# Forward 47-point stage on the quarters of the matrix array: groups of four points, plain float32

## The chip, the cores and the metric

The kernel runs on one core of one Trainium2 chip. A core has five engines with an instruction queue each: TensorE (PE in the profile, with its weight loads as PEld), VectorE (DVE), ScalarE (ACT), GpSimd (POOL) and SyncE (SP, which here only issues transfers). The metric is the device time of one execution in microseconds. The kernel before takes 2449.47 us (median of 3 runs, 2446.99 to 2450.57).

## The reference

Eight sequences `x[b]` of 3008 tokens by 256 channels are Fourier transformed along the tokens, mixed with a complex 256x256 matrix, shrunk towards zero, and transformed back. What comes out passes a token-mixing and a channel-mixing layer.

```python
X = np.fft.rfft(x, axis=1)
Yr = Xr @ w_r - Xi @ w_i + b_r
Yi = Xr @ w_i + Xi @ w_r + b_i
Yr = np.sign(Yr) * np.maximum(np.abs(Yr) - lam, 0.0)   # Yi alike
y = np.fft.irfft(Y, n=x.shape[1], axis=1)
...
h = np.maximum(xt @ w_tok1, 0.0) @ w_tok2
u = x + h.transpose(0, 2, 1)
h2 = np.maximum(u @ w_ch1, 0.0) @ w_ch2
return (u + h2).astype(np.float32)
```

## The kernel before

**Units.** 3008 is 47 times 64, so the transform is done as 47-point transforms at each of 64 residues n2 (stage one), and then 64-point transforms. The batches are worked in five units: batch 0 alone, batch 1 alone, and then three pairs (`UNITS`). A unit's work on the spectrum, `spectral(u)`, runs while the channel layer of the unit before it, `channel(n)`, keeps TensorE busy. Unit 0 has its own beginning, `begin`, in which stage one is done another way (`stage1_turned`).

**Stage one** (`dft47`, `stage1`). Since the input is real, each residue needs only sums and differences of rows j and 47-j: 24 cosine terms from the sums and 24 sine terms from the differences. Five residues ("points") make a group of 5 times 24 = 120 partitions, and one 120x120 block-diagonal constant `f1` does all five, once with cosines (i = 0) and once with sines (i = 1). 64 points need 13 groups. A group is 512 columns wide in a unit of two batches, 256 in unit 1. For each group: SP loads `x` (three buffers, loaded three groups ahead); POOL (DVE in unit 1) makes the sums and DVE the differences, `sd`; ACT copies `sd` into a rounded float32 `xh` (type float32r, which the matrix unit takes in one pass) and DVE makes the rest `xl = sd - xh`; then `mm3` (L185 to L188) does three float32r products each for cosines and sines, six in all, into two PSUM banks (one bank in unit 1); ACT copies the banks to `a` (L257) and issues its store to `a_d` in DRAM (L259). All matrix products whose lines are L186, L187 and L188 are such triples; plain float32 products stand at other lines, such as L337, L451, L475, L517 and L751.

**What sets the order.** The code records instructions through generators. `channel(n)` yields after each of its 14 slices, and the loop at the end then takes as many steps of `spectral(u + 1)` as a pace asks for: every step yields its cost (0.7 us per batch of a stage-one group), the pace is work left in `spectral` over work left in `channel`. A scheduling layer then sets the final place of each instruction in its engine's queue from operands and buffers; it may move products of one group apart. PSUM has four banks in rotation (`bank`) which stage one shares with the first product of the channel layer (`ph`), the mixing products and others. `make_w` (L337), which only the beginning uses, is the one place before the change where products use a part of the array: its constant has 64 columns, so its four float32 products of a step write the upper or the lower half of a bank, two and two.

## Time and profile before

| | before |
|---|---|
| median of 3 runs | 2449.47 us (2446.99 to 2450.57) |
| span of the profiled execution, first to last instruction | 2442.4 us |
| median less span, what lies around the span | 7.1 us |
| instructions | 31613 |
| PE busy | 2420.4 us, 99% |
| DVE, ACT, POOL busy | 1103.6, 875.3, 305.2 us |
| granted TensorE clock | 1.000 |
| stage-one rows on TensorE outside unit 0 and the weights | 234 with 512 columns, 78 with 256 |

The page gives the profiled execution's span and no other time of that execution, so 7.1 us is taken for what lies around the span in every run. A row of the profile has the line in the kernel, the engine, the operation and "out<-in" by the program's names with buffer numbers left out (a PSUM bank `p1` shows as `p`). One float32r product is one MATMUL row; one plain float32 product is two MATMUL rows, with a weight load each. A matmul's shown duration goes on after the next has begun, so what a product costs is read from the distance between starts, not from its duration.

### The profile page before, as it was taken

The page shows a single profiled execution, that of the slowest core. Times are in us where ns is not written, and L with a number is a line of the kernel's source. Part 1 is how long each engine was busy: PE and PEld are TensorE (multiplying, and loading weights), DVE is VectorE, ACT ScalarE, POOL GpSimd, SP SyncE. Part 2 cuts the span into 40 slices and gives each one's busy share as a digit, 9 for nine tenths or more (in the row PEclk, how much of TensorE's full clock was granted, in tenths as well). Part 3 has the DMA queues.
Part 4 walks back from the last instruction along what each step waited for, and adds up shares of the span by engine and source line. Part 5 has one row for each costly group of instructions (what it writes and reads, how often), then busy time and mean ns, then how long its engine had stood idle before and what let it go on. Part 6 is the DMA issues. An engine that isn't in the chain of part 4 may idle for free.

```text
span 2442.4 us, 31613 instructions
## 1 busy us (share of the span) xinstructions
PE 2420.4 (99%) x12848; PEld 2114.3 (87%) x12848; DVE 1103.6 (45%) x1680; ACT 875.3 (36%) x1580; POOL 305.2 (12%) x259
## 2 busy tenths in 40 slices
PE   8999999999999999999999999999999999999999
PEld 7778999988888888888888898888888888888887
DVE  7986655454445444433344353444334333232332
ACT  6764444443333343333333253333333222222221
POOL 0000223122222011111111120111111000000000
PEclk9999999999999999999999999999999999999999
DMA  8864335542324352223322363232321212112110
GB/s 216 254 210 141 102 111 160 167 138 93 100 86 131 112 170 72 60 80 91 89 75 69 98 177 105 68 99 76 93 67 37 70 50 64 59 49 81 37 56 18
DMA packets 143998, 246.07 MB, mean 101 GB/s; under 512 B 10293, under 2 KB 97677, under 8 KB 143853
## 3 DMA queue, kind: packets, MB, share of 16 engines
q1 hardware_dynamic: 114073, 190.57, 26.4%
q10 hardware_dynamic: 29780, 53.49, 7.0%
q8 instruction: 101, 1.65, 0.3%
q14 instruction: 44, 0.36, 0.0%
HBM read 159.74 MB, written 84.28 MB: 100 GB/s over the span
## 4 chain that ended last, share of the span: by engine, by line
PE 93%; DMA 2%; DVE 2%; ACT 1%; SPq 1%; issue 0%; POOL 0%; ACTq 0%; DVEq 0%; POOLq 0%
PE ph L186 10%; PE ph L187 10%; PE ph L188 10%; PE po L188 10%; PE po L186 10%; PE po L187 10%; PE pu L751 5%; PE px L451 3%; PE pm L186 2%; PE pm L188 2%; PE pm L187 2%; PE pu L186 2%; PE pu L187 2%; PE pu L188 2%; PE gp L186 2%; PE gp L188 2%
## 5 line engine op out<-in xcount | busy, mean ns | idle before, releaser
L790 DVE SCALAR_TENSOR_TENSOR hlo<-ph,hh 128x512 fp32r<-128x512 f32 (+4 forms) x588 | 392.0, 667 | 640.0 <-ACT hh L789 635.8
L789 ACT ACTIVATE hh<-ph 128x512 fp32r<-128x512 f32 (+4 forms) x588 | 340.9, 581 | 822.3 <-PE ph L188 820.2
L186 PE MATMUL ph<-uh,w 128*128 128x512 f32 (+4 forms) x1176 | 455.7, 388 | 0.9 <-DVE hlo L790 0.9
L187 PE MATMUL ph<-ul,w 128*128 128x512 f32 (+4 forms) x1176 | 449.1, 382 | 0.0
L186 PE MATMUL po<-hh,w2h 128*128 128x512 f32 (+4 forms) x1176 | 448.5, 381 | 0.0
L188 PE MATMUL ph<-uh,w 128*128 128x512 f32 (+4 forms) x1176 | 448.5, 381 | 0.0
L187 PE MATMUL po<-hlo,w2h 128*128 128x512 f32 (+4 forms) x1176 | 447.9, 381 | 0.0
L188 PE MATMUL po<-hh,w2l 128*128 128x512 f32 (+4 forms) x1176 | 447.8, 381 | 0.0
L188 PEld LDWEIGHTS ph<-uh,w 128*128 128x128 f32 x1176 | 220.8, 188 | 39.5
L187 PEld LDWEIGHTS po<-hlo,w2h 128*128 128x128 f32 x1176 | 220.9, 188 | 38.6
L186 PEld LDWEIGHTS po<-hh,w2h 128*128 128x128 f32 x1176 | 220.8, 188 | 38.5
L188 PEld LDWEIGHTS po<-hh,w2l 128*128 128x128 f32 x1176 | 220.8, 188 | 38.4
L186 PEld LDWEIGHTS ph<-uh,w 128*128 128x128 f32 x1176 | 221.2, 188 | 35.5 <-DVE hlo L790 1.3
L187 PEld LDWEIGHTS ph<-ul,w 128*128 128x128 f32 x1176 | 221.3, 188 | 34.0 <-DVE ul L760 0.2
L140 DVE TENSOR_TENSOR xtl<-xf,xth 128x768 fp32r<-128x768 f32 x84 | 80.5, 958 | 208.7 <-ACT xth L137 208.7
L186 PE MATMUL pm<-wmh,xth 128*128 128x256 f32 x504 | 144.4, 287 | 1.1 <-ACT xth L137 1.1
L758 ACT COPY uf<-pu 128x470 f32<-128x470 f32 (+23 forms) x188 | 62.7, 376 | 228.1 <-PE pu L751 228.1
L140 POOL TENSOR_TENSOR yl<-z,yh 128x512 fp32r<-128x512 f32 x72 | 92.9, 1290 | 408.6 <-ACT yh L137 408.6
L188 PE MATMUL pm<-wmh,xtl 128*128 128x256 f32 x504 | 142.4, 283 | 0.0
L187 PE MATMUL pm<-wml,xth 128*128 128x256 f32 x504 | 142.3, 283 | 0.0
L751 PEld LDWEIGHTS pu<-g,b 96*128 96x128 f32 x1024 | 130.8, 191 | 3.4
L454 POOL TENSOR_TENSOR xf<-xf 128x256 f32<-128x256 f32 x84 | 69.0, 821 | 484.8 <-ACT xf L453 483.3
(130 smaller groups left out, 3216.3 us busy)
## 6 DMA issues: line engine op xcount, KB each, us to landing
wt<-wt_d SPq DMA_DIRECT2D x28, 940.0 KB, 5.6
x<-in_x SPq DMA_DIRECT2D x39, 480.0 KB, 4.4
a<-a_d SPq DMA_DIRECT2D x36, 512.0 KB, 3.8
b_d<-bt ACTq DMA_DIRECT2D x36, 512.0 KB, 3.3
out<-o SPq DMA_DIRECT2D x34, 512.0 KB, 2.8
a_d<-a ACTq DMA_DIRECT2D x36, 480.0 KB, 3.4
wt<-wt_d SPq DMA_DIRECT2D x21, 752.0 KB, 5.2
b<-b_d SPq DMA_DIRECT2D x32, 480.0 KB, 6.3
```

What stands on the lines that cost most here:

```text
L140: lo_eng.tensor_tensor(out=lo, in0=src, in1=hi.bitcast(F32), op=ALU.subtract)
L186: PE.matmul(out, lhsT=wh, rhs=xh, start=start, stop=False)
L187: PE.matmul(out, lhsT=wh, rhs=xl, start=False, stop=False)
L188: PE.matmul(out, lhsT=wl, rhs=xh, start=False, stop=stop)
L451: PE.matmul(pt[:, o:o + 128], lhsT=x, rhs=f2cols(2 * kp + ab), start=True, stop=True)
L454: (V if plain else G).tensor_tensor(out=xf[:, 0], in0=xf[:, 1], in1=xf[:, 2], op=ALU.add)
L751: PE.matmul(pt[:, s * TOKS:(s + 1) * TOKS], lhsT=b2[:, s, cs], rhs=g2[:, 0 if s0 + s == 0 else 1], start=False, stop=s == k - 1)
L758: S.copy(out=ufs[m][:, ct, lo - at:hi - at], in_=pt[:, lo - c0:hi - c0])
L789: S.activation(out=hh, in_=pt, func=AF.Relu)
L790: V.scalar_tensor_tensor(out=hlo, in0=pt, scalar=0.0, in1=hh.bitcast(F32), op0=ALU.max, op1=ALU.subtract)
```

## The change

Stage one of units 1 to 4 works in groups of four points: 16 groups in place of 13. The four points are two pairs r = 0, 1. A pair's 48 rows lie at partitions 0 to 47 and 64 to 111, and the constant `fq` has 48 rows and 64 columns, so that a product uses a quarter of the 128x128 array: r picks the upper or the lower half of the rows, i (cosines or sines) the left or right half of the columns. The two r write two banks, the two i the two halves of a bank. The four products of a group (a "quad" from here on) are plain float32 from `sd` as it is; the split into `xh` and `xl` goes, and with it the constants `f1r`. A group's load is two transfers, its store two. Sums and differences are made one group ahead of the products where it was two. The step's cost in the pacing is 0.47 per batch where it was 0.7, and `left_s` 68.7 where it was 70.3. Stage one of unit 0 and of the weights keeps groups of five; their last group now overlaps the one before it, since the host's array has no padding.

```diff
-NG = 13
-GS = 5
+NG, GS = 16, 4
+NG5, GS5 = 13, 5
...
+    fq = np.zeros((2, 2, KH, 2, 2, 32))
+    for n in range(2):
+        fq[:, n, :, 0, n, :KH] = f1[:KH, 0, :KH]
+        fq[:, n, :, 1, n, :KH] = f1[:KH, 1, :KH]
...
-    f1r = const.tile([120, 2, 2, 128], F32R, name="f1r")
+    fq = const.tile([128, 2, 64], F32, name="fq")
...
-    split(f1r[:, 0], f1r[:, 1], f1w[:, :2], S, V)
...
-    def split_x(sd, w):
-        xh, xl = hl([120, 2, w], "xh"), hl([120, 2, w], "xl")
-        split(xh, xl, sd, S, V)
-        return xh, xl
+    def load_q(src, nb):
+        x = ld([128, 2, nb, C], "x")
+        for r in range(2):
+            n = (64, 2 * KH)[r]
+            DMA.dma_start(out=x[r * 64:r * 64 + n], in_=src[r * 2 * KH:r * 2 * KH + n])
+        return x.rearrange("q i b c -> q i (b c)")[:112]
+
+    def stage1_quads(x, dst, g, w, eng):
+        sd = t4([112, 2, w], "sd")
+        eng.tensor_tensor(out=sd[:, 0], in0=x[:, 0], in1=x[:, 1], op=ALU.add)
+        V.tensor_tensor(out=sd[:, 1], in0=x[:, 0], in1=x[:, 1], op=ALU.subtract)
+        yield
+        a = ev([128, 2, w], "a")
+        pts = [bank("p1") for _ in range(2)]
+        for i in range(2):
+            for r in range(2):
+                ks = slice(r * 64, r * 64 + 2 * KH)
+                PE.matmul(pts[r][i * 64:(i + 1) * 64, :w], lhsT=fq[ks, i], rhs=sd[ks, i], start=True, stop=True)
+        for r in range(2):
+            S.copy(out=a[:, r], in_=pts[r][:, :w])
+        rows = dst.rearrange("(i g r n) k w -> i g (n k) r w", i=2, r=2, n=2)
+        for i in range(2):
+            PUT.dma_start(out=rows[i, g, :, :, :w], in_=a[i * 64:i * 64 + 2 * KH])
+
+    def dft_quads(load, dst, w, eng):
+        xs = [load(g) for g in range(3)]
+        yield 0.0
+        ahead = []
+        for g in range(NG + 1):
+            if g < NG:
+                if g + 3 < NG:
+                    xs.append(load(g + 3))
+                q = stage1_quads(xs[g], dst, g, w, eng)
+                xs[g] = None
+                next(q)
+                ahead.append(q)
+            if g >= 1:
+                for _ in ahead.pop(0):
+                    pass
+                yield 0.47 * w / C
...
-        yield from dft47(p.load_unit, p.a, p.w, 3, V if u == 1 else G)
+        yield from dft_quads(p.load_unit, p.a, p.w, V if u == 1 else G)
...
+            DMA.dma_start(out=fq, in_=io["fq"])
...
-            left_s = len(UNITS[u + 1]) * 70.3 - done
+            left_s = len(UNITS[u + 1]) * 68.7 - done
```

**TensorE, unit 3, between the second half of one channel chunk's products.** `p_7895` and `p_7900` are the two banks of one group (cosines, sines), `ph` and `po` the channel layer's two products. Before:

```order
L187 MATMUL po<-hlo,w2h 128x384
L188 MATMUL po<-hh,w2l 128x384
L186 MATMUL p_7895<-xh,f1r 128x512
L187 MATMUL p_7895<-xl,f1r 128x512
L188 MATMUL p_7895<-xh,f1r 128x512
L186 MATMUL p_7900<-xh,f1r 128x512
L187 MATMUL p_7900<-xl,f1r 128x512
L188 MATMUL p_7900<-xh,f1r 128x512
L186 MATMUL po<-hh,w2h 128x384
```

A group's six products stand together, all on the whole array. With the change, at an earlier place of the same unit:

```order
L791 MATMUL pu<-g_72,b_7610 128x94 x5
L262 MATMUL p_7852<-sd,fq 64x512
L262 MATMUL p_7853<-sd,fq 64x512
L262 MATMUL p_7852<-sd,fq 64x512
L262 MATMUL p_7853<-sd,fq 64x512
L262 MATMUL p_7869<-sd,fq 64x512
L262 MATMUL p_7870<-sd,fq 64x512
L262 MATMUL p_7869<-sd,fq 64x512
L262 MATMUL p_7870<-sd,fq 64x512
L193 MATMUL ph<-uh,w_948 128x384
```

Two whole quads have come to stand next to each other (banks 7852 and 7853, then 7869 and 7870); whole-array products come before and behind.

**TensorE, the same unit, a little later, with the change.** Lines L193 to L195 are `mm3`.

```order
L195 MATMUL po<-hh,w2l 128x384
L262 MATMUL p_7970<-sd,fq 64x512
L194 MATMUL po<-hlo,w2h 128x384
L195 MATMUL po<-hh,w2l 128x384
L193 MATMUL po<-hh,w2h 128x384
L194 MATMUL po<-hlo,w2h 128x384
L195 MATMUL po<-hh,w2l 128x384
L262 MATMUL p_7971<-sd,fq 64x512
L262 MATMUL p_7970<-sd,fq 64x512
L262 MATMUL p_7971<-sd,fq 64x512
L193 MATMUL ph<-uh,w_948 128x512
```

Here the scheduling layer has taken one quad apart: one of its products, five products of the channel layer, and then its other three. Counted over the whole program, the 256 products of the 64 quads stand in 60 unbroken stretches, 47 with 512 columns and 13 with 256. If each stretch is counted as often as its most used quarter of the array has products, the 48 quads with 512 columns make 56 such counts, and the 16 with 256 make 20; the surplus is quads taken apart. If it is counted as often as the more used column half has products, both row halves together, the sums are 98 and 37.

**SP, unit 1's loads, with the change.** A bracket names the counters on which the issue waits: an engine's, or one of eight (DMAHW0 to DMAHW7) that the transfers of all queues signal in rotation.

```order
L249 DMA x<-in_x 64x2x256 [waits DVE_49]
L249 DMA x<-in_x 48x2x256
L249 DMA x<-in_x 64x2x256 [waits DMAHW1_49,DVE_49]
L249 DMA x<-in_x 48x2x256 [waits DMAHW2_49]
L249 DMA x<-in_x 64x2x256 [waits DMAHW5_49,DMAHW6_49,DMAHW0_49,DVE_49]
L249 DMA x<-in_x 48x2x256
L249 DMA x<-in_x 64x2x256 [waits DMAHW4_49,DVE_49]
L249 DMA x<-in_x 48x2x256 [waits DMAHW2_49]
```

Before, a group's load was one row, `L421 DMA x<-in_x 120x2x256`, with the same kinds of waits. Now it is two, the two stores of a group (on ACT's queue) take two more of the eight counters, and the wait for DVE is for the sums and differences of a group whose instructions were recorded just behind the load, where they were recorded two steps ahead of it.

## The prediction

> **What bounds the kernel now.** I read the page's first part, then the chain of waits, then busy time by stages, then the groups by shape.

> ```profile
> span 2442.4 us, 31613 instructions
> PE 2420.4 (99%) x12848; PEld 2114.3 (87%) x12848; DVE 1103.6 (45%) x1680; ACT 875.3 (36%) x1580; POOL 305.2 (12%) x259
> PE 93%; DMA 2%; DVE 2%; ACT 1%; SPq 1%; issue 0%; POOL 0%; ACTq 0%; DVEq 0%; POOLq 0%
> ```

> TensorE is busy 99% of the span and is 93% of the chain that ended last. A busy matrix engine may still be a pipeline waiting, so the stages decide:

> ```profile
> 145.00:200.00 55.00, 52.88 (x287) 46.87 (x286) 47.09 (x94) 33.09 (x63) 0.00 (x0) 1.00 0.63 192
> 200.00:250.00 50.00, 48.32 (x281) 43.30 (x279) 29.80 (x51) 20.64 (x36) 6.60 (x6) 1.00 0.38 113
> 390.00:620.00 230.00, 228.05 (x1301) 207.32 (x1300) 114.38 (x161) 96.61 (x172) 54.89 (x43) 1.00 0.46 140
> 620.00:1100.00 480.00, 480.00 (x2572) 419.71 (x2571) 217.14 (x302) 176.40 (x311) 89.01 (x76) 1.00 0.34 102
> 1450.00:1900.00 450.00, 450.00 (x2381) 389.56 (x2380) 185.59 (x262) 149.98 (x269) 63.47 (x57) 1.00 0.27 81
> ```

> Columns: stretch, length, then PE, PEld, DVE, ACT and POOL busy, granted clock, share of DMA, GB/s. Stage one lies in the first two rows (unit 1), the third (unit 2) and the last two (units 3, 4; its products are seen up to 1479 us). In the last two TensorE never rests, at full clock; in the others it lacks 2.1, 1.7 and 2.0 us. So a microsecond that stage one takes on TensorE is a microsecond of the kernel, and what DVE and ACT are spared is worth at most those few.

> **What is removed on TensorE.**

> ```profile
> L187 PE MATMUL p<-xl,f1r 120*128 120x512 f32 x78 | 30.8, 395 | 0.3 <-DVE xl L140 0.3
> L187 PE MATMUL p<-xl,f1r 120*128 120x256 f32 x26 | 7.6, 292 | 0.8 <-DVE xl L140 0.8
> 1460.26 0.40 PE L186 MATMUL p<-xh,f1r 120*128 120x512 f32 x1
> ...
> 1461.66 0.39 PE L186 MATMUL ph<-uh,w 128*128 128x512 f32 x1
> 191.48 0.28 PE L186 MATMUL p<-xh,f1r 120*128 120x256 f32 x1
> ...
> 192.19 0.38 PE L186 MATMUL ph<-uh,w 128*128 128x470 f32 x1
> ```

> The last four rows, from the timeline, are the first of a group's six products and what follows the sixth. A group costs 1461.66 - 1460.26 = 1.40 us with 512 columns and 0.71 with 256. The counts give 78 x 3 / 6 = 39 groups and 13. Removed: 39 x 1.40 + 13 x 0.71 = 63.8 us.

> **What is added on TensorE.** Nothing in the trace uses quarters. The nearest row is L337: plain float32, 64 columns of weights, two halves of the array.

> ```profile
> L337 PE MATMUL pw<-aw,fw 128*64 128x256 f32 x96 | 13.1, 392 | 0.9 <-DMA aw<-a_w 0.9
> 115.79 1.06 PE pi L502 x4
> 116.85 1.73 PE gp L517 x8
> 118.58 1.02 PE pw L337 x8
> 119.60 1.92 PE gp L517 x8
> 121.53 1.02 PE pw L337 x8
> 122.55 1.92 PE gp L517 x8
> ```

> The last six rows are the chain of waits. L517 is plain float32 with 256 columns on the whole array: eight rows (four products) in 1.73 us after another whole-array product, 0.216 us a row. Behind L337 the same eight take 1.92. One round, 119.60 to 122.55, is 2.95 us. Take off L517's 1.73, and four products of L337 cost 1.22. One after another they would be 8 x 0.216 = 1.73; two and two side by side 0.86. So the halves do run side by side, and coming into and out of that layout costs 1.22 - 0.86 = 0.36 us, split as the rows show it: 0.16 on entry (1.02 against 0.86), 0.19 on exit (1.92 against 1.73). I take 0.35 a stretch. All twelve of these steps stand between whole-array products, as quads do.

> [...]

> From 256 to 512 columns six products go from 0.71 to 1.40, times 1.97, so a float32 row with 512 columns takes 0.43. A quad, if all four quarters run at once, is two rows long: 0.86 us, or 0.43 with 256 columns. The part of the document on the change counts 60 stretches that hold 56 and 20 such quad times, because quads are taken apart (48 and 16 otherwise). A lone product holds the array as long as a whole quad, and a second stretch pays the visit again. Added: 56 x 0.86 + 20 x 0.43 + 60 x 0.35 = 48.2 + 8.6 + 21.0 = 77.8 us. **On TensorE: 77.8 - 63.8 = +14.0 us.**

> Bounds of the visit: below 0, if what follows or precedes hid it; above, if the quarters' first weight loads, two more than the halves', followed each other:

> ```profile
> L337 PEld LDWEIGHTS pw<-aw,fw x96: 132/137/138, 100.2 to 139.6; 128*64 128x64 f32 x96
> ```

> 0.35 + 2 x 0.137 = 0.62. That is -21 to +16 us round the sum. I take 0.35, since twelve of twelve visits show it.

> **Other engines.**

> ```profile
> L140 DVE TENSOR_TENSOR xl<-sd,xh 120x1024 fp32r<-120x1024 f32 x39 | 48.7, 1248 | 48.9 <-ACT xh L137 46.5 <-PE gp L188 2.4
> L137 ACT CAST xh<-sd 120x1024 fp32r<-120x1024 f32 x39 | 41.0, 1051 | 11.0 <-PE gp L187 10.4 <-PE gp L188 0.6
> L235 POOL TENSOR_TENSOR sd<-x 120x512 f32<-120x512 f32 x39 | 62.1, 1591 | 202.2 <-DVE xl L140 201.8
> L257 ACT COPY a<-p x104: 558/587/596, 33.6 to 1479.8; 120x512 f32<-120x512 f32 x104
> 1459.07 0.32 ACTq L259 DMA_DIRECT2D a_d<-a  x1
> L421 SPq DMA_DIRECT2D x<-in_x x65: 324/358/1029, 1.7 to 1449.5; - x65
> PE p L187 <- DVE xl L140: 1.1, 3, 0.4
> PE p L186 <- ACT a L257: 0.9, 1, 0.9
> ```

> DVE loses 49 us of `xl` and ACT 41 of `xh` in the pairs, and some less in unit 1. Added are nine groups of sums on POOL (9 x 1.6 = 14 us), 18 copies with 512 columns on ACT (10.6 us), and 128 - 52 = 76 issues each on ACT (24 us) and SP (27 us). All of it lies under TensorE; DVE in unit 1, the fullest at 47 of 55 us, gets lighter. If that cover were gone, each group would pay a copy and an issue more, about 0.9 us. In return the two waits in the last two rows, 1.1 + 0.9 = 2.0 us, go: there is no `xl`, and I count no like wait for `a`. The dropped split of `f1` at the start is one shorter `xl`, below 0.7 us under the first loads; I take nothing, nor for the load of `fq`.

> **The new wait.** A group's load waits for the sums and differences of the group three before, now recorded just behind it. Queued behind it on SP are the other half-load, `wt` and `b` for the next token group, and `out`; the first two are asked for six slices or more (16 us) ahead of use. What is late next is `x` itself:

> ```profile
> x<-in_x SPq DMA_DIRECT2D x26, 240.0 KB, 4.8
> 183.50 0.28 PE L186 MATMUL p<-xh,f1r 120*128 120x256 f32 x1
> 206.99 0.38 PE L186 MATMUL ph<-uh,w 128*128 128x470 f32 x1
> ```

> Ten groups of unit 1 ran in 23.5 us, 2.35 each. With four transfers of eight counters per group, only two groups are in flight in 4.8 us: 2.4 each. Thirteen of the 16 groups have to fit there, where 10 did; if the order is as dense as 2.0 us a group, 13 x 0.4 = 5 us are lost, if TensorE's order is as loose as before, none. I take the middle, +2.5.

> **Sum:** +14.0 - 2.0 + 2.5 = +14.5 us. Span 2442.4 + 14.5 = 2456.9; with the 7.1 around it **2464.0 us**, 0.6% slower. The profiled execution plus 7.1 is the median by construction.

> **Rivals.**

> *The visits cost nothing* (0.16). The 0.35 could belong to `make_w`: its weights change with every product, and its neighbours are plain float32, where quads stand between float32r products. Then the added time is 56.8, and 56.8 - 63.8 - 2.0 + 2.5 = -6.5: **2443.0 us**, faster. Decided at (63.8 + 2.0 - 2.5 - 56.8) / 60 = 0.11 us a visit. For it: the sum without visits is clearly below. Against it: the exit price shows on L517, whose weights are as wide as those of `ph` and `po`. [...]

> *Only column halves run side by side* (0.08). That is all that the trace shows; the two row halves could take turns. By the second count of the same part, 98 and 37: 98 x 0.86 + 37 x 0.43 + 21.0 = 121.2 us, +57.4, with the other terms **2507 us**. For it: no row with 64 rows or fewer. Against it: the two r read different partitions and write different banks. [...]

> *More waiting for buffers and loads* (0.16). Quads next to each other take four banks at once, and ACT empties a quad's two banks one after the other, 2 x 0.59 us, where the first could start halfway through the group. Eight-product stretches in units 1 and 2, and 5 us for loads in each of them rather than 2.5 in one: about +10: **2474 us**. For it: the 2.0 us of rest in 390 to 620. Against it: the lighter DVE and ACT.

> The change does what it says only in part: 12 surplus quad times and the extra visits are in the sum. Whole quads with free visits would give 48 x 0.86 + 16 x 0.43 = 48.2, the largest gain thinkable, -15.6.

> **How the numbers follow.** Forecast 0.60, rivals 0.16, 0.08, 0.16. The forecast's own range is 2455 to 2475 (visits from 0.25 to 0.5, waits 0 to 5). For 8 in 10 it must reach the free visit and the waits: 2441 to 2480, the upper end being the upper bound of the visit; left out are the row halves and the tails. A measurement of this kernel tells about 0.2%, 4.9 us, from no change. Faster: 0.15, nearly all from the first rival. Same: 0.07, visits near 0.11 to 0.2. Slower: 0.78.

> **What would show it.** In the new profile, L262 rows in the timeline: four starts close together, a second four 0.43 us later (0.22 in unit 1); the next `ph` or `po` about 1.2 us after the quad's first start, and its first row longer than its neighbours'. The stretches of units 3 and 4 stay filled to the last, so their length grows by the quads alone. `p` on L262 has 512 rows. If a quad takes 0.9 us from the row before it to the row behind it, the visit was wrong; if starts come two and two, row halves take turns; if TensorE rests over 5 us in 140 to 250 or 390 to 620, the loads.

## The result, and the profile after

| | before | after |
|---|---|---|
| median | 2448.23 us (2446.75 to 2450.57, 4 runs) | 2483.36 us (2479.80 to 2486.04, 4 runs) |
| ratio | | 1.0143, 95% interval 1.0130 to 1.0155 |
| span of the profiled execution | 2442.4 us | 2481.7 us |
| mean granted clock in it | 1.000 | 0.995 |

The change makes the kernel 35.1 us slower, where 14.5 were forecast. The predicted range was 2441 to 2480 us. The execution with the profile took 2483.56 us, so only 1.9 us lie around the span, not the 7.1 that the prediction took. Later runs of the kernel before have 2.0 around it too, so its profiled execution was one of its quicker ones, of about 2444 us. This does the forecast no harm, which was the median plus 14.5.

The page's first part and its chain, after:

```profile
span 2481.7 us, 32210 instructions
PE 2451.2 (99%) x13048; PEld 2082.0 (84%) x13048; DVE 1055.8 (43%) x1642; ACT 844.8 (34%) x1564; POOL 320.2 (13%) x268
PE 93%; DVE 3%; DMA 2%; ACT 1%; SPq 1%; issue 0%; POOL 0%; ACTq 0%; DVEq 0%; POOLq 0%
```

DVE lost 48 us and ACT 31, and neither shows as a gain. The share of TensorE is what it was, and hides the loss: the stages show it. The same five stretches as in the prediction (stretch, length, PE, PEld, DVE, ACT, POOL, granted clock, DMA share, GB/s):

```profile
145.00:200.00 55.00, 51.54 (x289) 39.77 (x288) 39.90 (x78) 27.43 (x59) 1.27 (x1) 1.00 0.57 169
200.00:250.00 50.00, 47.36 (x271) 37.17 (x270) 25.64 (x47) 18.83 (x40) 2.91 (x3) 0.97 0.48 143
390.00:620.00 230.00, 225.12 (x1309) 191.49 (x1308) 101.20 (x156) 85.92 (x164) 58.92 (x44) 0.97 0.49 144
620.00:1100.00 480.00, 479.85 (x2605) 404.08 (x2604) 201.81 (x294) 166.93 (x303) 97.46 (x81) 1.00 0.35 104
1450.00:1900.00 450.00, 449.85 (x2401) 377.52 (x2400) 177.76 (x254) 147.89 (x272) 75.28 (x62) 1.00 0.33 98
```

Two things are new in the first three rows. TensorE lacks 3.5, 2.6 and 4.9 us, where it lacked 2.1, 1.7 and 2.0. And the granted clock, 1.00 everywhere before, is 0.97 in two of them. In the records of the clock TensorE runs at half speed in four places: 3.4 us from 33 and from 101 us on, 3.4 from 217, and 13.7 from 514 to 527.7. The prediction did not think of the clock at all.

Where the time came in is read from rows that both kernels have. `hlo` is written 588 times by each; I compare the ends of the 1st, 79th, 143rd, 271st and last. The 79th, from the timelines of DVE, of before:

```profile
437.19 0.55 DVE L790 SCALAR_TENSOR_TENSOR hlo<-ph,hh 128x376 fp32r<-128x376 f32 x1 [1.53 <-ACT hh L789]
```

and after:

```profile
452.88 0.55 DVE L830 SCALAR_TENSOR_TENSOR hlo<-ph,hh 128x376 fp32r<-128x376 f32 x1 [1.53 <-ACT hh L829]
```

The forecast of each unit in this table is the prediction's own sum, with its 60 stretches and 56 + 20 quad times divided by units: 13 stretches and 20 short quad times in unit 1, 11 and 18 in unit 2, 36 and 38 in units 3 and 4 (13 x 0.35 + 20 x 0.43 - 13 x 0.71 = 3.9, and so on; it adds up to 13.9, which the prediction rounds to 14.0).

| later by, us | up to the first `hlo` | unit 1 | unit 2 | unit 3 | unit 4 | all |
|---|---|---|---|---|---|---|
| forecast, TensorE alone | 0 | 3.9 | 1.1 | 4.4 | 4.4 | 13.9 |
| measured | 3.0 | 12.6 | 11.7 | 5.8 | 5.9 | 39.1 |

So the two units in which TensorE hardly rests come near the forecast, and the two others take five times what was forecast. The first 3.0 us lie ahead of the quads: the last product of `make_w` already starts 4.0 us later (143.10 for 139.13). A half-clock stretch that begins between 23 and 42 us is in 14 of the 16 profiled executions of this document, that of lone, with the stage one of before, among them, and not in those of before and visits_before. The four units together are 36.0 us longer, the medians 35.1 apart.

**A quad and its visit** are as the prediction had them. From the timeline of TensorE in unit 3 after, a whole quad between two products of the channel layer:

```profile
863.70 0.33 PE L194 MATMUL po<-hlo,w2h 128*128 128x384 f32 x1
863.88 0.34 PE L195 MATMUL po<-hh,w2l 128*128 128x384 f32 x1
864.14 1.09 PE L262 MATMUL p<-sd,fq 48*64 48x512 f32 x8
865.16 0.44 PE L193 MATMUL ph<-uh,w 128*128 128x384 f32 x1
865.44 0.34 PE L194 MATMUL ph<-ul,w 128*128 128x384 f32 x1
```

From 863.88 to 865.44 are 1.56 us; two ordinary steps of 0.175 leave 1.21 for the quad, 0.86 and 0.35 for the visit. Inside the row of eight, the records start at 0, 7, 14, 20 and then at 480, 487, 494, 500 ns: four quarters at once, the second pass 0.48 us behind: 0.43, as between the two passes at 490.46 and 490.89 us, and 0.05, which I put down to the first loads. Coming in costs 0.09, going out 0.10 ahead of the next product and 0.10 in it.

**The rests.** The same view at the end of unit 2's stage one, behind the making of `u`:

```profile
505.56 1.09 PE L262 MATMUL p<-sd,fq 48*64 48x512 f32 x8
...
507.59 2.17 PE L262 MATMUL p<-sd,fq 48*64 48x512 f32 x16
...
510.71 1.09 PE L262 MATMUL p<-sd,fq 48*64 48x512 f32 x8 [0.34 <-POOL sd L254]
514.33 2.37 PE L262 MATMUL p<-sd,fq 48*64 48x512 f32 x8 [2.53 <-ACT a L264]
518.36 0.74 PE L193 MATMUL ph<-uh,w 128*128 128x448 f32 x1 [1.66 <-ACT a L264]
518.90 0.57 PE L194 MATMUL ph<-ul,w 128*128 128x448 f32 x1
519.27 0.57 PE L195 MATMUL ph<-uh,w 128*128 128x448 f32 x1
```

Five quads follow each other with six products between them. They wait first for a sum, then for ACT's copies out of the banks, with the clock at half from 514.1 (steps of 0.37 us where 0.20 is usual). The stretch in three pieces, by the windows:

```profile
480.00:505.00 25.00, 24.91 (x130) 15.69 (x129) 10.55 (x12) 10.16 (x19) 11.39 (x7) 1.00 0.95 259
505.00:514.00 9.00, 6.46 (x44) 2.27 (x43) 2.63 (x3) 3.10 (x6) 5.24 (x3) 1.00 1.02 297
514.00:527.70 13.70, 11.71 (x39) 6.21 (x40) 2.01 (x3) 5.51 (x11) 3.58 (x2) 0.50 0.60 175
```

The last two have 2.5 and 2.0 us of rest. 11.7 busy us at the clock of 0.50 would be 5.9 at full, an estimate from the clock, so 5.9 are lost; with the 1.1 of the forecast that is 11.5 of unit 2's 11.7. Two things that this leaves out nearly cancel. The stretches of two quads at 489.55 and 494.59 took 2.2 us more than their 2.07 each, while the windows show TensorE busy; and the kernel before rested 2.0 us in this unit too. In unit 1 the starts of the quarter products that come later than their pace add up to about 7 us, the 3.4 us at half clock lose 1.7, and the forecast had 3.9: together about the 12.6. What they and the copies waited for, from the view of waits (whole kernel; us, times, longest):

```profile
PE p L262 <- ACT a L264: 4.0, 2, 2.5
PE p L262 <- DVE sd L254: 2.5, 3, 1.5
ACT a L264 <- DMA a_d<-a: 28.0, 12, 3.8
```

ACT's copy itself waits for the stores that free the two `a` buffers. That was the first theory for the experiments: the store buffers, or the four banks, are too few. The issues from 505 to 513 us show how slow these stores are there (KB each, median us from issue to landing):

```profile
wt<-wt_d SPq DMA_DIRECT2D x1, 940.0 KB, 6.4
a_d<-a ACTq DMA_DIRECT2D x4, 192.0 KB, 5.3
b<-b_d SPq DMA_DIRECT2D x1, 480.0 KB, 6.8
```

Over the whole kernel the median of such a store is 3.0. Here the loads for the next token group, `wt` and `b`, are under way beside those of x, at a DMA share of 1.02, and the copies go on within 0.1 us of a landing.

### The profile page after: what moved, and what is told of

Read it like the earlier page. It is cut to its first block, busy times and chain, and to the rows that moved or that the text cites. A ratio compares the mean times of both kernels' runs of the same rounds, so it can differ in the third digit from the quotient of the medians.

```text
span 2481.7 us, 32210 instructions
## 1 busy us (share of the span) xinstructions
PE 2451.2 (99%) x13048; PEld 2082.0 (84%) x13048; DVE 1055.8 (43%) x1642; ACT 844.8 (34%) x1564; POOL 320.2 (13%) x268
## 4 chain that ended last, share of the span: by engine, by line
PE 93%; DVE 3%; DMA 2%; ACT 1%; SPq 1%; issue 0%; POOL 0%; ACTq 0%; DVEq 0%; POOLq 0%
PE ph L193 11%; PE ph L194 10%; PE ph L195 10%; PE po L193 10%; PE po L194 10%; PE po L195 10%; PE pu L791 4%; PE px L490 3%; PE p L262 2%; PE pm L193 2%; PE pm L195 2%; PE pm L194 2%; PE pu L193 2%; PE pu L194 2%; PE pu L195 2%; PE gp L193 2%
## 5 line engine op out<-in xcount | busy, mean ns | idle before, releaser
L193 PE MATMUL ph<-uh,w 128*128 128x512 f32 (+4 forms) x1176 | 460.6, 392 | 1.7 <-ACT a L264 1.7
L193 PE MATMUL po<-hh,w2h 128*128 128x512 f32 (+4 forms) x1176 | 450.5, 383 | 0.0
L195 PE MATMUL ph<-uh,w 128*128 128x512 f32 (+4 forms) x1176 | 449.1, 382 | 0.0
L195 PE MATMUL po<-hh,w2l 128*128 128x512 f32 (+4 forms) x1176 | 449.0, 382 | 0.0
L193 PEld LDWEIGHTS ph<-uh,w 128*128 128x128 f32 x1176 | 221.8, 189 | 63.2 <-issue 20.6
L193 PEld LDWEIGHTS po<-hh,w2h 128*128 128x128 f32 x1176 | 221.1, 188 | 47.9 <-issue 5.3
L195 PEld LDWEIGHTS po<-hh,w2l 128*128 128x128 f32 x1176 | 221.2, 188 | 41.7 <-issue 2.8
L195 PEld LDWEIGHTS ph<-uh,w 128*128 128x128 f32 x1176 | 221.4, 188 | 39.5
L193 PE MATMUL pm<-wmh,xth 128*128 128x256 f32 x504 | 144.8, 287 | 0.2 <-ACT xth L144 0.2
L195 PE MATMUL pm<-wmh,xtl 128*128 128x256 f32 x504 | 142.4, 283 | 0.0
L791 PE MATMUL pu<-g,b 96*128 96x94 f32 x1024 | 129.2, 271 | 0.0
```

Source lines behind the costliest of these rows:

```text
L193: PE.matmul(out, lhsT=wh, rhs=xh, start=start, stop=False)
L195: PE.matmul(out, lhsT=wl, rhs=xh, start=False, stop=stop)
L791: PE.matmul(pt[:, s * TOKS:(s + 1) * TOKS], lhsT=b2[:, s, cs], rhs=g2[:, 0 if s0 + s == 0 else 1], start=False, stop=s == k - 1)
```

## The experiments

The table has the times; each ratio is to the kernel before on the same chip. In the last six columns, how much later than before the same `hlo` rows end, as above, and how long TensorE was at half clock, each from one profiled execution. Such a figure is not sharp to less than 2 us in units 1 and 2: unit 1 came to 12.6 in the change and to 14.8 in fewx2, which has the same unit 1 in the same order.

| kernel | median, us | ratio (95%) | start | unit 1 | unit 2 | unit 3 | unit 4 | half clock, us |
|---|---|---|---|---|---|---|---|---|
| the change | 2483.4 | 1.0143 (1.0130 to 1.0155) | 3.0 | 12.6 | 11.7 | 5.8 | 5.9 | 24 |
| visits_before | 2462.8 | 1.0056 (1.0033 to 1.0078) | 1.7 | 2.4 | 2.9 | 5.3 | 5.3 | 0 |
| gp2 | 2479.5 | 1.0123 (1.0101 to 1.0145) | -0.7 | 14.1 | 16.2 | 1.5 | 1.5 | 34 |
| a4 | 2487.7 | 1.0156 (1.0133 to 1.0178) | 0.9 | 13.4 | 14.7 | 7.4 | 5.8 | 27 |
| old1 | 2469.2 | 1.0079 (1.0061 to 1.0097) | 3.3 | -0.7 | 10.7 | 5.8 | 5.9 | 17 |
| sup | 2479.3 | 1.0127 (1.0104 to 1.0150) | 6.1 | 8.5 | 7.2 | 6.0 | 5.4 | 17 |
| spread | 2472.3 | 1.0093 (1.0078 to 1.0108) | 1.5 | 8.4 | 10.8 | 3.4 | 3.4 | 14 |
| old12 | 2462.4 | 1.0060 (1.0040 to 1.0080) | 5.2 | -0.9 | 3.0 | 7.3 | 5.8 | 14 |
| lone | 2474.4 (1 run) | | 1.6 | -0.8 | 1.5 | 17.3 | 10.4 | 20 |
| rings | 2475.6 | 1.0121 (1.0104 to 1.0138) | 2.9 | 11.0 | 5.0 | 6.0 | 5.4 | 14 |
| ringsspread | 2473.9 | 1.0110 (1.0095 to 1.0125) | 3.2 | 5.8 | 10.5 | 4.7 | 4.1 | 14 |
| ringsgp2spread | 2465.7 | 1.0078 (1.0063 to 1.0093) | 2.7 | 8.2 | 1.8 | 5.1 | 4.5 | 7 |
| pair2 | 2463.0 | 1.0067 (1.0050 to 1.0084) | 9.6 | 7.4 | 0.8 | 0.8 | 0.3 | 20 |
| fewx2 | 2484.3 | 1.0147 (1.0130 to 1.0164) | 4.2 | 14.8 | 8.0 | 5.8 | 5.9 | 24 |
| fewx12 | 2475.0 | 1.0113 (1.0098 to 1.0128) | 6.1 | 7.0 | 6.1 | 5.8 | 5.9 | 17 |

**The price of a visit alone (visits_before).** The kernel before, with one tiny product on a quarter ahead of each group:

```diff
             pt = bank("p1")
+            if pool is None and i0 == 0:
+                PE.matmul(pt[:64, :32], lhsT=f1[:48, 0, :64], rhs=f2[:48, 0, :32], start=True, stop=True)
```

> The kernel before, with one more product in each of the 52 stage-one groups of units 1 to 4: plain float32 on one quarter of the array, 48 rows, 64 columns, 32 columns wide, into a bank that the group's own products then overwrite (its result is not used). 52 visits to the quarter layout with next to no work in them. Theory A (a visit costs 0.35 us, as L337 showed; the rest of the 35 us came from waiting and from a lower clock in units 1 and 2): 52 x (0.35 + two short rows, about 0.06) = 21 us, 2470 us. Theory B (between float32r products a visit costs more, about 0.7, which would account for all 35 us with 60 visits): 52 x 0.75 = 39 us, 2487 us. If visits were free: under 4 us, 2451 us.

From its timeline, in unit 4:

```profile
1465.61 0.40 PE L188 MATMUL ph<-uh,w 128*128 128x512 f32 x1
1465.94 0.30 PE L251 MATMUL p<-f,f 48*64 48x32 f32 x2
1466.16 0.50 PE L186 MATMUL p<-xh,f1r 120*128 120x512 f32 x1
1466.50 0.39 PE L187 MATMUL p<-xl,f1r 120*128 120x512 f32 x1
```

0.89 us from the first to the last row, 0.43 more than two ordinary steps of 0.23. In units 3 and 4, 26 visits cost 10.6 us, 0.41 each, of which about 0.06 is the product itself; in units 1 and 2 the other 26 cost 5.3. There 2.4 us of the rests of before are gone (4.3 us in the two units, now 1.9); what hides the rest of the price is not shown. So the whole, 12.8 us in the medians, is less than the 21 forecast. A visit between float32r products costs 0.35, as between the products of `make_w`, and the rival with free visits is refuted. The clock stayed full throughout the profiled execution (1.0): visits alone did not lower it.

**One tile of two banks for a quad (gp2), four store buffers (a4), unit 1 as before (old1).**

```diff
-        pts = [bank("p1") for _ in range(2)]
+        if w == 512:   # gp2
+            pq = ps1.tile([128, 2, 512], F32, tag="gp", name="p1")
+            pts = [pq[:, 0], pq[:, 1]]
+        else:
+            pts = [bank("p1") for _ in range(2)]
...
-        a = ev([128, 2, w], "a")
+        a = wk.tile([128, 2, w], F32, tag="hl", name="a", bufs=4)   # a4
...
+        yield from dft47_old(p.load_unit, p.a, p.w) if u == 1 else dft_quads(p.load_unit, p.a, p.w, G)   # old1
```

> The changed kernel; in units 2 to 4 a quad writes one two-bank tile (the two banks that hold the token sums in the second half of a unit, idle in stage one) in place of two banks of the shared four. The order then has all 48 quads of these units whole: 48 quad times where there were 56; the visits stay 47. Theory A: 8 x 0.86 = 7 us less, 2476 us, and a little less where banks were waited for. Theory B: visits are as many as before and a quad's own time is not what is off, so the same 7 us; a larger gain (15 us or more) would say that the shared banks made the waiting.

> The changed kernel with four buffers for a group's result on its way to DRAM where there were two (they share the four that the dropped xh and xl used). Nothing else is edited; the order gets 65 stretches in place of 60, and 59 and 20 quad times in place of 56 and 20, which costs 3 x 0.86 + 5 x 0.35 = 4 us. Theory A: the wait for stores in units 1 and 2 and the half-clock stretch behind it in unit 2 go, about 4 + 7 us, net 4 to 8 us less, 2475 to 2479 us, with no half-clock stretch at 514 us. Theory B: no gain, 2484 to 2488 us.

> The changed kernel with stage one of unit 1 as before the change (13 groups of five points, split, three float32r products); the quads' constant is loaded when unit 2 begins. Theory A: unit 1 lost 12.7 us of 39 in the profile by the distance between like instructions of the two traces, of which 4.0 were in my sum; all of it comes back: 2471 us. Theory B: only unit 1's 13 visits at 0.7 and its quads come back: 13 x 0.7 + 8.6 - 9.2 = 8.5 us, 2475 us.

With gp2 every quad of units 2 to 4 stays whole, and units 3 and 4 fall from 5.8 and 5.9 to 1.5 each. Of the 7 us forecast only 3.9 come in the medians, since unit 2 gets worse, by a wait behind the last quads:

```profile
PE px L494 <- DMA a<-a_d: 8.4, 1, 8.4
PE p L266 <- ACT a L268: 2.8, 1, 2.8
```

With a4 the waits in unit 2 (from 440 to 640 us) only change their name, from the copies to the sums:

```profile
PE p L262 <- POOL sd L254: 3.3, 3, 1.6
PE p L262 <- ACT a L264: 1.5, 1, 1.5
```

So more store buffers alone do not help: the time is in the range of theory B, though the order, with more quads taken apart, was expected to cost 4 us by itself. With old1 unit 1's part comes back (14 us in the medians), and most of unit 2's loss stays, 10.7: each unit's loss is its own.

**A longer supply (sup), a wider plan (spread), quads in units 3 and 4 alone (old12).** `sup` gives x five buffers, the sums four and makes them two groups ahead; `spread` changes the plan; in `old12` stage one of units 1 and 2 is that of before:

```diff
-        x = ld([128, 2, nb, C], "x")
+        x = (ld if g % 5 < 3 else t4)([128, 2, nb, C], "x")   # sup
...
-        sd = t4([112, 2, w], "sd")
+        sd = wk.tile([112, 2, w], F32, tag="hl", name="sd", bufs=4)   # sup
...
-                yield 0.47 * w / C
+                yield 0.7 * w / C   # spread
...
-            left_s = len(UNITS[u + 1]) * 68.7 - done
+            left_s = len(UNITS[u + 1]) * 72.4 - done   # spread
...
+        yield from dft47_old(p.load_unit, p.a, p.w, V if u == 1 else G) if u <= 2 else dft_quads(p.load_unit, p.a, p.w, G)   # old12
```

> The changed kernel with a longer supply to the quads: five buffers for x in place of three, four for the sums and differences in place of two, sums made two groups ahead in place of one; the stores keep their two buffers. The quads are the same (47 stretches with 512 columns, 16 with 256). Theory A (where groups come close together in units 1 and 2, TensorE rests for the sums, and they for x): the rests inside and behind the quads' stretches, 6.9 us in unit 1 and 5.3 in unit 2 of the changed kernel, shrink to less than half, the clock has less cause to halve there (7.6 us lost now), and the time is 2466 to 2473. Theory B (it is the stores and the two copies out of the banks that set the rate there): the same rests stand behind the copies (ACT a), and the time stays at 2478 to 2490.

> The changed kernel with one thing different in the plan: a group of quads is planned as 1.4 us of TensorE's work (as a group of five points was) in place of 0.94, so that fewer groups are put next to each other, above all behind the making of u, where the plan catches up. Theory C (the groups are planned too close together, at 0.94 us for a quad that takes 0.86 and 0.41 for its visit): the rests in units 1 and 2 shrink by more than half, with them the half clock, and the time is 2465 to 2474, though there are some more visits (51 stretches for 47). Theory D (the supply is too slow even for groups so far apart): less than 4 us change, 2479 to 2488.

> Units 1 and 2 as before the change (groups of five points, six products), only units 3 and 4 with quads. In the changed kernel units 3 and 4 each took 5.9 us more, without rests. If the quads' and visits' price is all that they cost where nothing waits, and the waits and the half clock of units 1 and 2 the rest: 11.8 us over the kernel before, 2460 (2457 to 2463), at full clock from 100 us on. If part of what is lost in units 1 and 2 only moves into unit 3, over 2465.

`sup` misses its forecast: unit 1 gains 4 us, unit 2 4.5, the start loses 3, and the longest rest in unit 2 is now again the copies'; the time, 2479.3, is in the range of theory B. `spread` gains 11 us, within its forecast, but only half of it where it was expected: 4.2 in unit 1, 0.9 in unit 2, and 2.4 in each of units 3 and 4, where the quads come apart less (17 stretches for 18). The time of `old12` is as forecast, 14 us above before, but not at full clock. Its units 3 and 4 take 13.1 us more, with 3.4 us at half clock in unit 3, 1.7 lost; without that 11.4, for 8.9 by the prediction's sum. Another 3.4 us at half clock, from 499.6 on, are in its unit 2, which has no quads: the clock can halve there without them.

**Does the clock follow rest, or the work of the array (lone).** The kernel before, with two stretches of useless products:

```diff
+            if extra and i0 == 0:   # ahead of one group of unit 3 (48 rows, 64 columns) and of unit 4 (120, 128)
+                for _ in range(24):
+                    m = 64 if extra == 48 else 128
+                    PE.matmul(pt[:m, :256], lhsT=f1w[:extra, 0, :m], rhs=f2.rearrange("p a b -> p (a b)")[:extra, :256], start=True, stop=True)
```

> The kernel before, with 24 float32 products of 48 rows and 64 columns of weights on 256 columns, all on one quarter of the array, put ahead of one group of unit 3, and 24 products of 120 rows and 128 columns on 256 columns ahead of one group of unit 4; their results are written over. Each row of 24 needs nothing that is late and takes about 24 x 0.43 = 10.4 us. Theory E (the clock follows the share of the array that computes, taken over stretches of 3.4 us): it halves in or right behind the first row of 24, though TensorE does not rest, and not in the second; unit 3 then takes some 15 to 20 us more than before, unit 4 some 10. Theory F (the clock follows rest alone): full clock in both, 10 to 11 us more in each.

The two stretches in the timeline:

```profile
855.36 15.30 PE L258 MATMUL p<-f,f 48*64 48x256 f32 x48
...
1459.74 10.52 PE L258 MATMUL p<-f,f 120*128 120x256 f32 x48
```

and windows round them:

```profile
850.00:861.00 11.00, 11.00 (x61) 8.13 (x60) 3.75 (x4) 3.26 (x7) 1.77 (x1) 1.00 0.80 226
861.00:874.70 13.70, 13.70 (x34) 8.31 (x33) 0.45 (x1) 2.11 (x3) 0.00 (x0) 0.50 0.10 33
...
1460.00:1472.00 12.00, 12.00 (x57) 10.53 (x56) 2.85 (x3) 2.29 (x4) 1.77 (x1) 1.00 0.60 184
```

TensorE is busy without a gap in all three. In the quarter the clock halves 5.6 us after the first product, at 861.0, and stays so until 4 us after the last; the whole array keeps its clock. Unit 3 takes 17.3 us more, unit 4 10.4. So it is not rest alone that halves the clock: 24 single products on one quarter brought it to 0.50 with TensorE busy, and as many on nearly the whole array left it at 1.00. In this execution, too, the clock is at half for 3.4 us in unit 2, from 495.7 on, where nothing was changed.

**Both rings, with the plan and with whole quads (rings, ringsspread, ringsgp2spread).**

```diff
-        sd = t4([112, 2, w], "sd")
+        sd = wk.tile([112, 2, w], F32, tag="hl", name="sd", bufs=4)
...
-        a = ev([128, 2, w], "a")
+        a = (ev, t4)[g % 2]([128, 2, w], "a")
...
-        for g in range(NG + 1):
+        for g in range(NG + 2):
...
-            if g >= 1:
+            if g >= 2:
```

> The changed kernel with longer rings at both ends of a quad: sums and differences two groups ahead in four buffers, and four buffers for the stores; x keeps its three, and the plan its 0.94 us a group. Quad times by its order of work: 8.2 us with 256 columns, 50.7 with 512, in 64 stretches at 0.41 us: 85 us, 21 more than the six products took. Theory A (the rests of units 1 and 2 are two rings of two buffers, in turn the sums' and the stores'; longer stores alone only moved the rest to the sums, longer sums alone to the stores): with both, the rests in these units fall below 3 us each, and the time is 2463 to 2470. Theory C alone (the plan puts the groups too close together, and no ring of four helps, since x still comes in three buffers): 2477 to 2488.

> As the kernel with longer rings at both ends, and a group planned as 1.4 us in place of 0.94. Quads 7.3 + 49.0 us, 63 stretches at 0.41: 82 us, 18 more than the six products. Theories A and C together (too close a plan and too short rings are two sides of one shortage): rests below 2 us in each of units 1 and 2, no half clock there, 2461 to 2468. If the plan alone was the cause, the rings add nothing: 2470 to 2475, as with the plan alone.

> As the one before, and in units 2 to 4 the two banks of a quad are one tile of two banks, so that more of its quads stay whole: 7.3 + 44.7 us, 64 stretches at 0.41: 78 us, 14 more than the six products, 4.3 less than with single banks. Theory A: 2457 to 2465, the least that groups of four points with a visit each can do here. If one tile of two banks for each quad makes the quads wait for the copies out of it, as it did without the longer rings: no gain on the kernel without it, or slower.

With rings, unit 2 falls to 5.0; the end of its stage one, which had 13.7 us at half clock, is filled and at full clock:

```profile
480.00:505.00 25.00, 24.82 (x135) 14.82 (x133) 6.38 (x10) 9.59 (x18) 11.16 (x7) 1.00 0.89 260
505.00:527.70 22.70, 22.70 (x133) 15.00 (x126) 5.59 (x8) 10.77 (x23) 5.25 (x3) 1.00 0.63 187
```

The time, 2475.6, lies between the ranges of the two theories nevertheless, since unit 1 loses 11.0 (6.8 us at half clock from 205 on). Rings and plan together, 2473.9, are no better than the plan alone, where 2461 to 2468 was the forecast if both were at fault, and unit 2 is back at 10.5, with 6.8 us at half clock. There the copies stood behind ACT's own issue of two stores:

```profile
500.71 4.35 ACTq L267 DMA_DIRECT2D a_d<-a  x2
```

4.35 us where 0.79 is usual, at a DMA share of 1.08 (the column before the last) from 500 to 505:

```profile
500.00:505.00 5.00, 2.85 (x18) 1.26 (x14) 1.93 (x2) 1.17 (x3) 3.22 (x2) 1.00 1.08 306
```

With the tiles of two banks as well, units 2, 3 and 4 are at 1.8, 5.1 and 4.5, and the time, 2465.7 us, is just above its forecast of 2457 to 2465. All quads of unit 2 are whole there; in units 3 and 4 one each is still taken apart.

**Two quads a visit (pair2).** As the last, with two groups at a time, their quads one behind the other.

```diff
+        pq = ps1.tile([128, 2, 512], F32, tag="gp", name="p1") if w == 512 else None
+        pts = [[bank("p1") for _ in range(2)], [pq[:, 0], pq[:, 1]] if w == 512 else [bank("p1") for _ in range(2)]]
```

> As the kernel with the longer rings, the wider plan and two-bank tiles, but two groups are taken at a time: their two quads are put one behind the other (the first in two single banks, the second in one two-bank tile in units 2 to 4), so that one coming and going serves both. By its order 41 stretches in place of 64, with 7.8 + 45.6 us of quads in place of 52.0. Theory A (the visit is paid once a stretch, at 0.41 us, and rests stay small): 23 x 0.41 - 1.4 = 8 us less than with single quads, 2455 to 2460, about 8 to 10 us above the kernel before. If what is paid is not a stretch's coming and going but goes with the number of quarter products: within 2 us of the single quads, 2463 to 2468. If two groups at a time wait more for sums, banks and stores: above 2468.

In unit 3:

```profile
863.42 0.34 PE L195 MATMUL po<-hh,w2l 128*128 128x384 f32 x1
863.69 1.95 PE L267 MATMUL p<-sd,fq 48*64 48x512 f32 x16
865.57 0.44 PE L193 MATMUL ph<-uh,w 128*128 128x384 f32 x1
865.85 0.33 PE L194 MATMUL ph<-ul,w 128*128 128x384 f32 x1
```

2.43 us less 0.35 are 2.08 for two quads and one visit, 2 x 0.86 + 0.36. Units 2, 3 and 4 come down to 0.8, 0.8 and 0.3 us above before: nine stretches in each of units 3 and 4, 18 in the changed kernel. So the visit goes with the stretch, not with the products; this rests on the rows and the units, since the median itself, 2.7 us less and not 8, is at the edge of the other theory's range and not clear of noise. The start and unit 1 lose 17.0 us together (10.9 with single quads), with all 20 us of half clock there. No version that I ran beats the kernel before.

**Are the DMA engines the cause (fewx2, fewx12).** Three of four loads of x are left out in unit 2, or in units 1 and 2; those groups work on the x of the group ahead.

```diff
+                if g % 4 == 0:
+                    wc["x4"] = load_q(src[:, :, bs[0] % 2:bs[0] % 2 + nb], nb)
+                return wc["x4"]
```

> The changed kernel, but in unit 2 only every fourth group loads its x, and the three groups behind it use the same x (so three quarters of unit 2's input is left out: 5.4 MB less to move, 12 x 448 KB). Stores, rings, plan and order of the quads stay (60 stretches, the same quad times). Theory G (in unit 2's stage the DMA engines are full, and the stores that free the two store buffers land late for that): rests and half clock of unit 2 go, its 11.7 us fall to 1 to 4, the time is 2472 to 2476. Theory B (two store buffers, two banks a quad and ACT's copies set the rate, however free the DMA engines are): unit 2 keeps 8 us or more, 2479 to 2487.

> As the one before, in unit 1 too. Unit 1's stage has a DMA share of 0.6 to 0.8, so not full, but its sums waited for x. Theory G for unit 2 and late x in unit 1: unit 1's 12.6 us fall to 4 to 6 as well, 2464 to 2469. If unit 1's rests come from the copies out of the banks and the order: 2471 to 2476, as with unit 2 alone.

Unit 2 gains 3.7 us in fewx2, not the 8 to 10 of theory G, and keeps 8.0, as theory B had it. From its windows:

```profile
480.00:510.00 30.00, 29.91 (x167) 18.14 (x170) 11.81 (x14) 13.10 (x25) 14.57 (x9) 1.00 0.54 148
510.00:515.00 5.00, 3.57 (x26) 0.71 (x18) 2.81 (x3) 1.17 (x3) 4.75 (x4) 1.00 1.07 334
```

Up to 510 us the share of DMA is 0.54 where it was 0.95, and the rest comes all the same, behind the copies, which wait 2.98 us for a store. But this does not clear the DMA engines. From 510 to 515 their share is 1.07 without any x: `wt` and `b`, issued at 506.7 and 507.8, are under way, and the two stores that the copies wait for, issued at 509.9 and 510.3, take 4.4 and 4.5 us, where 2.7 is the median of such a store in this run; the next copy starts at 514.90, 0.1 us after the second landing. So fewx2 took away only one of the loads that fill the engines there, and no run here takes away the others. In fewx12 unit 1 falls from 12.6 to 7.0, so there late x may be about half of the loss; the order of unit 1's products moved as well (13 stretches for 11).

**What follows.** I found no single limit that sets the rate of close groups. By estimates from the rows, three are near each other. The two store buffers: two copies take 1.07 us, the issues 0.8, the landing 3.0 (`a_d<-a`, the page's median), 4.9 us a buffer, 2.4 a group; with the 5.3 of the crowded place, 7.2 a buffer, 3.6 a group. The DMA engines: 448 KB of x and 384 KB of `a` a group, 832 KB, 2.9 us at the 297 GB/s of the full window. The three x buffers: 4.4 us to land and 1.8 for POOL's sum, 2.1 a group. The five quads from 505.56 on, with their three visits and the six products between them, are 4.3 + 1.05 + 1.2 = 6.5 us of TensorE, 1.3 us a group. So lifting one limit gains little or meets the next (for unit 2: a4 -3.0, that is worse, sup +4.5, fewx2 +3.7), rings +6.7, but with the plan as well +1.2, and rings, two-bank tiles and the plan together +9.9 of 11.7. What part of it is each one's can't be told from these runs, since most edits also move the order of the quads; and a window at half clock more or less, 1.7 us, comes with such small moves.

## Why the prediction was wrong, and what in it was right

**What bounds the kernel: right.** Units 3 and 4 stayed filled (479.85 of 480, 449.85 of 450 us), and 48 us taken off DVE show as no gain.

**Removed, quads, visits: right, but for units 3 and 4.** The price of a visit, 0.35, is in the rows of the change (0.35), of visits_before (0.35 to 0.38) and of pair2 (0.36). All four quarters run at once (their starts are 7 ns apart), so the rival in which row halves take turns is refuted, as is that of free visits. The TensorE sum was 8.9 us for units 3 and 4, and 11.7 came. 2.4 of the 2.8 is one stretch in each unit (at 885 and 1478 us) with two products of a quad taken apart, which run one behind the other, 2.2 us for a stretch that takes 1.0 where both run at once. The row of unit 4 names what the second waited for:

```profile
1478.18 1.07 PE L262 MATMUL p<-sd,fq 48*64 48x512 f32 x2
1479.41 1.07 PE L262 MATMUL p<-sd,fq 48*64 48x512 f32 x2 [0.15 <-DVE sd L255]
```

It is the difference, which the second product, a sine, reads. DVE had the channel layer's `ul` first (2.26 us from 1475.40), then two differences of this stage. So even here a quad waits for its sums and differences, which the change records only one group ahead, and it hardly shows as rest.

**"The new wait", "I take the middle, +2.5": wrong, and this is the step that failed.** Together with "there is no `xl`, and I count no like wait for `a`", -2.0, it makes waiting worth 0.5 us. Take the TensorE sum (3.9 and 1.1) and the half clock (1.7 and 5.9) off what units 1 and 2 lost, and 7.0 and 4.7 us are left: 11.7 us for waits, over what the kernel before waited there. The waits for `xl`, 1.1 us, did go; that for `a`, 0.9, became 4.0. Three things went wrong. The wait was worked out for unit 1 and x alone, though the order of work for unit 2 showed stretches of eight products, which the prediction used in a rival. It compared a rate of loads (2.4 us a group) with the rate before (2.35), and took the middle of 0 and 5 us, where groups in a bunch come every 1.3 us. And it never set the stores beside them, whose row was in the trace of before:

```profile
ACT a L257 <- DMA a_d<-a: 11.8, 8, 3.2
```

The same wait is 28.0 us after.

**The clock: missing, a second term at nothing.** 7.6 us (1.7 in unit 1, 5.9 in unit 2) are lost at half clock. No row of before showed less than 1.00 in these stages, so nothing there could be priced. lone shows that quarter products bring the clock down without a rest; lone and old12 show that unit 2 can come to half clock without quads (3.4 us in each). So the waits, the quads taken apart and the stage as it was before may all have a part in it, and how much is each one's stays open.

**"More waiting for buffers and loads", at 0.16:** the right places, units 1 and 2, and part of the mechanism, four banks and ACT's copies in turn; the stores behind the copies are not in it. Its 10 us were half of the 19 that the forecast was short of. The parts are then 13.9 for TensorE, 11.7 for waits, 7.6 for the clock and 2.8 more in units 3 and 4, 36.0 us for the four units; that they add up shows nothing, since the waits are what is left over.

**What would show it:** the list pointed to the place. "TensorE rests over 5 us in 140 to 250 or 390 to 620" came true: 6.1 us in 145 to 250, and 4.9 in 390 to 620 by the windows, for 3.8 and 2.0 before. The cause that it named, the loads, is only a part of it.

## What to carry to other kernels

Price a change of layout by its visits, not by its products: 0.35 us here for every coming and going, so that 16 quads of 0.86, which save 4.4 us a unit against 13 groups of 1.40, lose 6.3 again by 18 visits and 2.6 by the quads taken apart, and only two quads a visit came out nearly even (0.3 to 0.8 us). Where a plan sets pieces by their time on TensorE, compare the closest spacing that it makes with the time a piece needs in each thing that it goes through (loads, buffers, banks, stores) in the stage where the plan is tightest; take the landing time of the crowded stretch, not the median; and when several of these are as slow, mending one shows little. And look at the granted clock by stage: in lone, products on one quarter, with TensorE busy throughout, brought it to 0.50.

## What the runs showed of the hardware that was not expected

The four products of a quad start 7 ns apart, and a pass of a float32 product on a quarter takes as long as on the whole array: with 256 columns 0.216 us on the whole array (L517) and 0.214 on a quarter (from 211.071 to 211.285 us in unit 1 of the change), and 0.43 with 512 on a quarter, twice as long for twice the columns. So a quarter product alone is a quarter of a quad's work in a quad's time.
